# The attention residual of three row tiles: an identity product on TensorE, or a ScalarE copy and a GpSimd add

## The chip, the cores and the metric

The kernel runs on one core of a Trainium2 chip. Five engines share the core's on-chip memory (SBUF): TensorE (PE, matrix products, which write to PSUM), VectorE (DVE), ScalarE (ACT), GpSimd (POOL) and SyncE (SP, which here only issues transfers). Each works through its own instructions in the order of the program and waits on semaphores for the others. The metric is the device time of one execution in microseconds (us).

## The reference

A transformer block, forward only, on x of 2048 rows and 640 columns, followed by its gradients. The outputs are the block's result and the gradients of x and of all weights with respect to a given `grad_out`.

```python
x = A_x
h = x + _A_ref(_layernorm(x), A_wqkv, A_wo)      # linear attention, 32 heads of 20
h2 = h + _B_ref(_layernorm(h), B_w1, B_w3, B_w2) # silu(gate) * up, F = 1728
_out, _vjp = jax.vjp(_f, A_x, A_wqkv, A_wo, B_w1, B_w3, B_w2)
_grads = _vjp(grad_out)
```

The change is in how the first of the two residual sums, `h = x + attention`, is made for some of the rows. Matrix operands are bf16, sums in PSUM are f32, h is kept in bf16.

## The kernel before

The 2048 rows are 16 row tiles of 128 (`t` = 0 to 15), or 4 chunks of 512 rows (`c` = 0 to 3, four row tiles each). A row tile's 640 columns are handled in two halves of 320 (`j` = 0, 1; `HD` = 320).

The work is written in stages. The first makes q, k and the attention's small matrices. Then comes the stage that matters here: `f2_at` (line 634) makes the attention's result of a row tile, five matmuls per half into a PSUM tile `at` (line 642), adds x and writes h over x in `x_sb`. `ln2.part` (line 144) then takes statistics of that half (`bn_stats`, line 147), after the second half aggregates them (line 150), adds epsilon (line 153), and has GpSimd raise the sum to the power -0.5 (line 154). `f2_hn` normalizes the row tile on VectorE (line 160) and stores it; `f2_ht` transposes it for the MLP.

How x is added depends on the row tile:

- tiles 0 to 3, first half, tile 4, and tiles 8 to 15: VectorE adds x to the PSUM tile (line 649);
- tiles 0 to 3, second half, and tiles 5 to 7, both halves: a sixth matmul with the identity puts x into the PSUM sum (line 640), and ScalarE copies the sum to `x_sb` (line 647).

The MLP runs over the four chunks. `mlp(c, fc, between)` (line 762) does one of 14 column blocks: a matmul set of five for `gate`, one for `up`, and one for a later block of the gradient (`ghh_chunk`, line 390), each into a PSUM tile `mm` of which there are four. ScalarE empties them: sigmoid into `sig` and `s2` (lines 772, 773), copies into `up` and `gate` (lines 779, 783) and into `ghh` (line 406). These five SBUF tiles hold a pair of blocks. `sig`, `s2`, `gate` and `up` have two buffers each, so that ScalarE fills one pair while VectorE multiplies the other. For each pair VectorE does seven products or sums (line 808), queued in a list and let out one by one between other work. Three of their results go to DRAM (line 791): `hhT` by SP's queue, `gate` and `ghh` by GpSimd's queue, as `gg_d`. A `gate` buffer can be written again only when its store has landed.

While chunk c is multiplied, the row tiles of chunk c + 1 are prepared in between: `sides` (line 883) says after which block `f2_at`, `f2_hn` and `f2_ht` of each run. Tiles 5, 6 and 7 are therefore made in the first chunk, c = 0, in the blocks fc = 3, 6 and 8. The order of every engine's instructions is the order in which this program records them; no scheduler moves them.

The buffers of tag `h2` (two of 128 rows) serve several short-lived tiles: products of a row tile in the attention stage, the normalized rows of tile 3, and from chunk 1 on the block's results before they are stored.

Of the kernel before, what the change touches and what calls it, by code (L numbers as in the profile page):

```python
# [9 lines left out]
P = 128  # L10
BF16 = mybir.dt.bfloat16
F32 = mybir.dt.float32
ALU = mybir.AluOpType
# [10 lines left out]
W, SC, TPC = 512, 4, 4  # L24
HD = D // 2
# [30 lines left out]
def kernel(  # L56
# [19 lines left out]
    V, A, T, G, SY = nc.vector, nc.scalar, nc.tensor, nc.gpsimd, nc.sync  # L76
# [27 lines left out]
    def pool(name, side="left", space=None):  # L104
        kw = dict(space=space) if space is not None else dict(side=side)
        return tc.alloc_tile_pool(name=name, bufs=1, reuse_waits="tile", **kw)
# [68 lines left out]
    pf = pool("pf", "right")  # L175
# [457 lines left out]

    def f2_at(t, tag="at", halves=(0, 1), hold=False):
        for j in halves:
            on_pe = t < 2 * TPC and (t > TPC or (t < TPC and j == 1))
            at = ps.tile([P, 512], F32, name="at", tag=tag, bufs=2)
            xs = x_sb[:, t, j * HD:(j + 1) * HD]
            if on_pe:
                T.matmul(at[:, 0:HD], lhsT=ident[:], rhs=xs, start=True, stop=False)  # L640
            for c in range(DT):
                T.matmul(at[:, 0:HD], lhsT=pqT[:, c, t * P:(t + 1) * P], rhs=Wp[:, c, j * HD:(j + 1) * HD],  # L642
                         start=(c == 0 and not on_pe), stop=(c == DT - 1))

            def rest(at=at, xs=xs, j=j, on_pe=on_pe):
                if on_pe:
                    A.copy(out=xs, in_=at[:, 0:HD])
                else:
                    V.tensor_tensor(out=xs, in0=at[:, 0:HD], in1=xs, op=ALU.add)
                ln2.part(x_sb, t, j)  # L650

            at_rest.append(rest)
            if not hold:
                f2_rest()

    def f2_rest():
        while at_rest:
            at_rest.pop(0)()
# [185 lines left out]
    def f2_at0(t):  # L844
        f2_at(t, "o2")

    def f2_half(t, j, hold=False):
        f2_at(t, ("o2", "at")[t % 2], (j,), hold)
# [34 lines left out]
    def sides(c):  # L883
        side = ({}, {})
        for i in range(TPC):
            k0 = 3 * i - (i == TPC - 1) * (1 + (c == 1)) + (-2, 1, 0)[c]
            for k, pos, f in ((k0 + 2, 1, f2_at), (k0 + 3, 0, f2_hn), (k0 + 3, 1, f2_ht)):
                if c == 0 and f is f2_at:
                    if i == 0:
                        continue  # L890
                    f = f2_at0
                if k0 == -2 and f in (f2_at0, f2_hn, f2_ht):
                    k, pos = (k + 1, 0) if f is f2_at0 else (k + 1, pos)
                if k >= 0:
                    side[pos].setdefault(k, []).append((f, i))
        return side
# [610 lines left out]
```

## Time and profile before

| | |
|---|---|
| median of 3 runs | 823.75 us (823.6 to 826.96) |
| span of the profiled execution, first to last instruction | 821.9 us |
| the profiled execution's own time | not on the page beside its span; the median run is 1.85 us above that span |
| TensorE clock granted | 1.00 in every stretch looked at |
| PE busy | 814.4 us (99%) |
| DVE, ACT, POOL busy | 453.1 us (55%), 325.0 us (40%), 133.1 us (16%) |
| matmuls with the identity (line 640) | 10, of which 6 for tiles 5 to 7, at 107.1 to 125.2 us |
| ScalarE copies of tiles 5 to 7 (line 647) | 6, 0.425 to 0.606 us |

A line of the timeline has the start in us from the span's start, the duration, the engine, the source line, the operation, what it writes and reads, the shapes, and in brackets the engine's idle time before it with what ended it. "DMA gg_d<-gate" as releaser is the landing of a transfer. A line of a group has a count and the least, median and greatest duration in ns. Instructions of one engine overlap a little at their ends, so that starts are the better measure of their spacing. The page counts 5549 weight loads and 5522 matmuls; each matmul has its own load, so 27 matmuls have no record.

### The profile page before, as it was taken

How to read it: one execution, taken by the hardware profiler on the slowest of the kernel's cores; microseconds unless marked ns; L12 is line 12 of the kernel's file. 1: busy time of each engine (PE TensorE's matmuls, PEld its weight loads, DVE VectorE, ACT ScalarE, POOL GpSimd, SP SyncE). 2: the span in 40 equal slices, each digit the busy share in tenths (PEclk: the TensorE clock that was granted, in tenths of full speed). 3: DMA queues.
4: the chain of work that ended last, by engine and by line, in shares of the span. 5: the costliest groups of instructions: out<-in, count | busy, mean ns of one | idle time of the engine just before them, and what ended most of it. 6: DMA issues, size and time to landing. Idle time of an engine off the chain costs nothing.

```text
span 821.9 us, 14179 instructions
## 1 busy us (share of the span) xinstructions
PE 814.4 (99%) x5522; PEld 522.6 (64%) x5549; DVE 453.1 (55%) x961; ACT 325.0 (40%) x609; POOL 133.1 (16%) x194
## 2 busy tenths in 40 slices
PE   8999999999999999999999999999999999999998
PEld 6677544555555555777777777767777777555554
DVE  7869887999898566300057777772681545200000
ACT  7856688665565666011122212222212334211111
POOL 2243333323223212100001111110220000000000
PEclk9999999999999999999999999999999999999999
DMA  9999889696485556999677897258984898885771
GB/s 233 254 279 227 207 234 312 196 242 157 145 213 155 166 181 162 250 241 267 195 170 179 206 204 188 70 113 178 268 216 93 164 200 181 201 199 137 165 170 38
DMA packets 320883, 157.26 MB, mean 191 GB/s; under 512 B 238704, under 2 KB 314064, under 8 KB 320816
## 3 DMA queue, kind: packets, MB, share of 16 engines
q1 hardware_dynamic: 278768, 115.54, 61.3%
q0 software_dynamic: 7328, 24.48, 8.9%
q10 hardware_dynamic: 34720, 16.34, 8.7%
q8 instruction: 43, 0.70, 0.4%
q14 instruction: 24, 0.20, 0.1%
HBM read 47.01 MB, written 51.13 MB: 119 GB/s over the span
## 4 chain that ended last, share of the span: by engine, by line
PE 94%; DVE 2%; ACT 1%; DMA 1%; issue 0%; SPq 0%; POOL 0%; DVEq 0%; ACTq 0%
PE mm L386 20%; PE job L1271 20%; PE ghn L1070 14%; PE gxn L1429 8%; PE o L833 7%; PE gw L1025 7%; PE gwo L1155 3%; PE big L266 3%; PE gr L1127 3%; PE dkv L1375 3%; PE macc L416 2%; PE at L642 2%; DMA wqkv<-in_A_wqkv_dram 1%; PE dkv L1303 1%; DVE st L147 1%; DMA Wp<-pkx 1%
## 5 line engine op out<-in xcount | busy, mean ns | idle before, releaser
L1271 PE MATMUL job<-gb,hnN 128*128 128x432 bf16 (+2 forms) x656 | 117.0, 342 | 0.0
L1070 PEld LDWEIGHTS <-ggb 128*128 128x128 bf16 x864 | 84.5, 98 | 32.8
L1271 PEld LDWEIGHTS <-hnN 128*128 128x128 bf16 x656 | 63.6, 98 | 53.4
L386 PE MATMUL mm<-pqT,w 128*128 128x512 bf16 x397 | 93.1, 379 | 0.5
L386 PEld LDWEIGHTS <-w 128*128 128x128 bf16 x540 | 52.5, 98 | 63.1 <-issue 0.8
L1275 ACT CAST obs<-job 128x432 bf16<-128x432 f32 (+3 forms) x61 | 29.3, 480 | 123.1 <-PE job L1271 123.1
L833 PE MATMUL o<-w,hhT 128*128 128x320 bf16 x448 | 67.7, 299 | 0.1
L1070 PE MATMUL ghn<-w13a,ggb 128*128 128x320 bf16 x448 | 63.5, 299 | 0.0
L1070 PE MATMUL ghn<-w13b,ggb 128*128 128x320 bf16 x416 | 61.4, 299 | 0.0
L386 PE MATMUL mm<-g2T,w2T 128*128 128x512 bf16 x227 | 58.5, 379 | 0.6
L833 PEld LDWEIGHTS <-hhT 128*128 128x128 bf16 x448 | 43.8, 98 | 23.8 <-issue 0.2
L1025 PE MATMUL gw<-g,hb 128*128 128x320 bf16 x416 | 56.8, 299 | 0.0
L1135 POOL TENSOR_TENSOR sz<-Zb,g_h 128x640 f32<-128x640 bf16 x16 | 20.2, 1260 | 198.8 <-DVE g_h L1133 107.7
L1025 PEld LDWEIGHTS <-hb 128*128 128x128 bf16 x416 | 40.6, 98 | 16.0 <-issue 0.3
L1429 PE MATMUL gxn<-wqT,gT 128*128 128x320 bf16 x320 | 48.7, 299 | 0.0
L406 ACT CAST ghh<-mm 128x512 bf16<-128x512 f32 x48 | 28.3, 590 | 44.7 <-PE mm L386 39.0
L772 ACT ACTIVATE sig<-mm 128x512 bf16<-128x512 f32 x56 | 33.9, 605 | 25.1 <-PE mm L386 21.6
L1082 ACT ACTIVATE gs<-ghn 128x640 bf16<-128x640 f32 x16 | 11.2, 703 | 78.9 <-PE ghn L1070 73.4
L386 PEld LDWEIGHTS <-w2T 128*128 128x128 bf16 x260 | 25.4, 98 | 23.3
L266 PEld LDWEIGHTS <-pqT 128*128 128x128 bf16 x320 | 30.6, 98 | 14.4 <-issue 1.7
L1429 PEld LDWEIGHTS <-gT 128*128 128x128 bf16 x320 | 31.3, 98 | 12.2
L266 PE MATMUL big<-wqkv,pqT 128*128 128x320 bf16 x250 | 38.5, 299 | 0.3
(210 smaller groups left out, 1282.3 us busy)
## 6 DMA issues: line engine op xcount, KB each, us to landing
hh_d<-hhT SPq DMA_DIRECT2D x24, 256.0 KB, 2.8
gg_d<-gate POOLq DMA_DIRECT2D x24, 256.0 KB, 4.1
gg_d<-ghh POOLq DMA_DIRECT2D x24, 256.0 KB, 3.5
ggb<-gg_d SPq DMA_DIRECT2D x6, 896.0 KB, 5.4
ggb<-gg_d ACTq DMA_DIRECT2D x6, 832.0 KB, 5.7
out_dram<-obs ACTq DMA_DIRECT2D x39, 108.0 KB, 3.0
x_sb<-in_A_x_dram SPq DMA_DIRECT2D x6, 640.0 KB, 5.4
ggb<-gg_d SPq DMA_DIRECT2D x2, 1728.0 KB, 13.5
```

Of the source, the lines that this page charges most:

```text
L266: T.matmul(acc, lhsT=pqT[:, c, t * P:(t + 1) * P], rhs=wqkv[:, c, n0:n0 + HD], start=(c == 0), stop=(c == DT - 1))
L386: T.matmul(acc[:], lhsT=w[:, c, fc * P:(fc + 1) * P], rhs=rhs[:, c, :], start=(c == 0), stop=(c == DT - 1))
L406: A.copy(out=ghh[n // 2][:, n % 2, :], in_=acc[:])
L772: A.activation(sig[:, i, :], gp[:], AF.Sigmoid)
L833: T.matmul(o2["ps"][:, 0:HD], lhsT=hhT[c][:, fc, i * P:(i + 1) * P], rhs=w2[:, fc, j * HD:(j + 1) * HD], start=(fc == 0), stop=(fc == FT - 1))
L1025: T.matmul(acc[:, j, 0:HD], lhsT=hb[b][:, t, i * P:(i + 1) * P], rhs=g2[:, t, j * HD:(j + 1) * HD], start=(t == 0), stop=(t == ST - 1))
L1070: T.matmul(acc[:, j, 0:HD], lhsT=ggb[t // 2][:, k, lo:lo + P], rhs=rhs[:, j * HD:(j + 1) * HD], start=(k == 0), stop=(k == NG - 1))
L1127: T.matmul(gr[t][:, j, 0:HD], lhsT=ghT[t][:, c, :], rhs=wT2[:, c, j * HD:(j + 1) * HD], start=(c == 0), stop=(c == DT - 1))
L1155: T.matmul(acc[m][:, j, 0:n], lhsT=r_sb[:, t, m * P:(m + 1) * P], rhs=g_hx[:, t, j * HD:j * HD + n], start=(t == 0), stop=(t == ST - 1))
L1271: T.matmul(acc[:, 0:n], lhsT=lhs[:, t, m * P:(m + 1) * P], rhs=rhs(t), start=(t == 0), stop=(t == ST - 1))
L1275: A.copy(out=ob, in_=acc[:, 0:n])
L1429: T.matmul(acc[:, j, 0:HD], lhsT=g, rhs=wqT[:, k, j * HD:(j + 1) * HD], start=(k == 0), stop=(k == 14))
```

## The change

For row tiles 5, 6 and 7 the matmul with the identity is gone. ScalarE copies the PSUM sum of the attention alone, as f32, into a new tile `af`, which takes the buffers of tag `h2`. GpSimd adds `af` and x and writes h to `x_sb`. The rest, tiles 0 to 3 among it, stays. `G.tensor_tensor` is GpSimd's operation on two tiles, as `V.tensor_tensor` is VectorE's.

```diff
     def f2_at(t, tag="at", halves=(0, 1), hold=False):
         for j in halves:
-            on_pe = t < 2 * TPC and (t > TPC or (t < TPC and j == 1))
+            on_pe = t < TPC and j == 1
+            on_g = TPC < t < 2 * TPC
             at = ps.tile([P, 512], F32, name="at", tag=tag, bufs=2)
             xs = x_sb[:, t, j * HD:(j + 1) * HD]
             if on_pe:
...
-            def rest(at=at, xs=xs, j=j, on_pe=on_pe):
+            def rest(at=at, xs=xs, j=j, on_pe=on_pe, on_g=on_g):
                 if on_pe:
                     A.copy(out=xs, in_=at[:, 0:HD])
+                elif on_g:
+                    af = pf.tile([P, HD], F32, name="af", tag="h2", bufs=2)
+                    A.copy(out=af[:], in_=at[:, 0:HD])
+                    G.tensor_tensor(out=xs, in0=af[:], in1=xs, op=ALU.add)
                 else:
                     V.tensor_tensor(out=xs, in0=at[:, 0:HD], in1=xs, op=ALU.add)
                 ln2.part(x_sb, t, j)
```

## The prediction

> **What bounds the kernel now.** I read the page first, then the groups of instructions of the tiles that the change touches, then the timeline of each engine around row tiles 5 to 7, and last the busy time by stretches.
>
> ```profile
> span 821.9 us, 14179 instructions
> PE 814.4 (99%) x5522; PEld 522.6 (64%) x5549; DVE 453.1 (55%) x961; ACT 325.0 (40%) x609; POOL 133.1 (16%) x194
> PE 94%; DVE 2%; ACT 1%; DMA 1%; issue 0%; SPq 0%; POOL 0%; DVEq 0%; ACTq 0%
> ```
>
> TensorE (PE) is busy for 99% and carries 94% of the chain that ended last, so a matmul less is a gain of its issue time and a TensorE stall is a loss one for one. GpSimd (POOL) has 84% of its time free; what counts is who waits for it.
>
> The stretches (after the window: busy us of PE, weight loads, VectorE (DVE), ScalarE (ACT), POOL, each with its count; clock; DMA share; GB/s) show the cover behind the change:
>
> ```profile
> 98.00:120.00 22.00, 21.89 (x110) 10.87 (x111) 19.16 (x38) 16.39 (x33) 8.15 (x12) 1.00 0.87 216
> 120.00:142.00 22.00, 21.89 (x112) 10.48 (x113) 18.49 (x34) 18.80 (x39) 7.64 (x11) 1.00 1.06 308
> 142.00:164.00 22.00, 21.89 (x119) 11.65 (x119) 19.85 (x41) 15.06 (x28) 6.94 (x11) 1.00 0.67 212
> 164.00:186.00 22.00, 21.84 (x118) 11.71 (x120) 21.48 (x45) 13.44 (x25) 6.39 (x9) 1.00 0.93 241
> ```
>
> Tiles 5, 6 and 7 lie at 107, 116 and 124 us, in MLP chunk 0. VectorE has 2 to 4 us idle per 22 us there and half a microsecond from 164 to 186: what it loses it regains slowly. The clock is 1.00 throughout.
>
> The timeline of the three engines at tiles 5 to 7 (start, duration, engine, line, out<-in, idle before and its releaser):
>
> ```profile
> 110.06 0.71 POOL L791 DMA_DIRECT2D gg_d<-ghh  x1 [1.03 <-DVE ghh L808]
> 114.30 0.74 POOL L791 DMA_DIRECT2D gg_d<-gate  x1 [1.68 <-ACT up L779]
> 126.86 0.72 POOL L791 DMA_DIRECT2D gg_d<-gate  x1 [2.53 <-ACT x_sb L647]
> 133.84 0.72 POOL L791 DMA_DIRECT2D gg_d<-gate  x1 [3.33 <-ACT gate L783]
> ...
> 119.71 0.58 ACT L783 CAST gate<-mm 128x512 bf16<-128x512 f32 x1 [2.61 <-DMA gg_d<-gate]
> 120.19 0.76 ACT L647 CAST x_sb<-at 128x320 bf16<-128x320 f32 x2
> 140.32 0.58 ACT L783 CAST gate<-mm 128x512 bf16<-128x512 f32 x1 [0.84 <-DMA gg_d<-gate]
> ...
> 110.28 0.88 DVE L147 BATCH_NORM_STATS2 st<-x_sb 128x6 f32<-128x320 bf16 x2
> 111.19 0.21 DVE L150 BATCH_NORM_AGGREGATE ln_mv<-st 128x2 f32<-128x12 f32 x1
> 120.66 0.89 DVE L147 BATCH_NORM_STATS2 st<-x_sb 128x6 f32<-128x320 bf16 x2 [1.59 <-ACT x_sb L647]
> 126.83 0.88 DVE L147 BATCH_NORM_STATS2 st<-x_sb 128x6 f32<-128x320 bf16 x2
> ```
>
> Two ScalarE copies already wait for something in POOL's queue: `gate` at 119.71 and at 140.32 waits until the store of an earlier `gate` has landed, because that tile has two buffers. A store issued later makes those copies later by as much.
>
> **The change part by part.** It takes six identity matmuls from TensorE (one per half of tiles 5 to 7). ScalarE's six copies stay and write f32 into a buffer of tag h2, whose last readers were done before 102 us. It adds six GpSimd adds. The matmul sets, stores and copies keep their order on every queue; on POOL each pair of adds stands behind the `gg_d` store that precedes it, on VectorE the same `bn_stats` now waits for the adds.
>
> *Identity products.* In the timeline a 128x320 matmul follows the one before by 0.135 us (the identity at 107.08, the next at 107.21). Six times 0.135 is 0.81 us, four of them (0.54) before 117.9, two (0.27) after 124.
>
> *ScalarE's copies.* They took a median of 0.43 us with a bf16 output. With f32 no row shows them; the bound below is no change, the bound above the 128x512 copy's 0.59, which is 0.16 each. I take no change, as the input and the element count stay.
>
> *The add.* No row shows it. The nearest are these groups (median ns in the middle):
>
> ```profile
> L358 POOL TENSOR_TENSOR pr<-pql,Zb x8: 777/787/792, 67.3 to 85.7; 128x320 f32<-128x320 bf16 x8
> L1135 POOL TENSOR_TENSOR sz<-Zb,g_h x16: 1252/1260/1262, 424.8 to 551.4; 128x640 f32<-128x640 bf16 x16
> L649 DVE TENSOR_TENSOR x_sb<-at,x_sb x22: 474/476/491, 87.1 to 258.0; 128x320 bf16<-128x320 f32 x22
> ```
>
> From below 0.476 (VectorE's own add of the same size), from above 1.26 (GpSimd with twice the elements); I take 0.787, the same engine, shape and number of inputs.
>
> *Tile 5.* POOL issues the `ghh` store at 110.06 for 0.71, then the adds run from 110.80 to 111.59 and 112.38. `bn_stats` of the second half can start at 112.42 and takes 0.49; the aggregate moves from 111.19 to 112.92, so VectorE is 1.7 late. Behind it stands the product whose result the next `gate` store carries: 114.30 becomes 116.0. That store landed at 119.63 before; everything that shares the DMA engines with it is issued behind VectorE too, on SP's and POOL's queues alike, so I keep its 5.33 us: 121.35. ScalarE's `gate` at 119.71 becomes 121.43, and the copies queued behind it (two of tile 6, ghh, sig, s2, up) move with it, as ScalarE has no idle time until 126.
>
> *TensorE's stall.* The matmul set at 121.13 uses the PSUM buffer that this `gate` copy releases (at 120.30, 0.83 before). Without four identities TensorE is there at 120.59 and waits for 122.02 plus 0.07: 0.97 late. The set at 122.21 waits for the ghh copy (end 121.45, then 123.17): 1.03 late. The set at 123.29 waits for the up copy (end 122.92, then 124.64): 1.42 late. Tile 7's two identities give 0.27 back: 1.15.
>
> *Tile 6.* Its copies end at 120.63 and 120.96 before, 122.35 and 122.68 after; the adds run to 124.02, the aggregate moves from 121.58 to 124.56: VectorE is 3.0 late. Its idle 1.59 us there was ScalarE's wait, which moves along.
>
> *Tile 7.* The `gate` store at 126.86 moves by 3.0 to 129.86, 0.72 later the adds start, they end at 132.2, and the aggregate moves from 127.75 to 132.76: 5.0 late. VectorE waits for these two adds over 2 us, with seven products of the next pairs queued behind.
>
> *What is late next.* The pair's product into ghh (128.78 to 129.47) ends at 134.5 and releases the s2 buffer that ScalarE wants at 133.3 (132.13 plus 1.15); TensorE had 1.0 us in hand, 0.26 more late: 1.41. VectorE's idle 0.71 us ahead of 130.54 absorbs as much, 4.3 remain. The store at 133.84 becomes 138.1, lands after its 6.4 us at 144.5 (140.24 before), and the `gate` copy at 140.32 ends at 145.2. TensorE's set at 141.88 had 0.98 in hand behind it and starts at 145.27: 3.39 late. In chunk 1 VectorE has almost no idle time; a PSUM tile that VectorE empties at 191.5 had 0.16 us in hand: I add 0.5 for this and a smaller such wait near 158.
>
> *Sum.* -0.81 (identities) + 1.96 (122 to 125 us) + 0.26 + 1.98 (145 us) + 0.5 = +3.9 us. The profiled execution has a span of 821.9 us; the median run is 823.75, 1.85 above, which I leave as it is. So 821.9 + 3.9 + 1.85 = 827.65, or 0.47% more. Each pair of adds is in line three times on the way to the store at 138.1, so a microsecond on one add is up to six: 0.476 gives +2.0, 1.26 gives +6.7. 0.16 on each ScalarE copy would be at most 0.3 per tile, 0.9 in all.
>
> The Trainium skill (GPSIMD Engine Reference, Engine selection) advises against this placement: an elementwise add of two tiles belongs on VectorE, GpSimd being about twice as slow. The rows above give 1.65 times (0.787 against 0.476). By the page's factor an add would be 0.95 as an estimate, and the sum +4.9 instead of +3.9. It prices the instruction alone; here the wait behind the queue costs more than the ratio.
>
> **The rivals.**
>
> *Only the first stall costs* (0.17). VectorE's lateness is made up before 133.84, so that only tile 5's effect reaches TensorE: +1.15, 824.9 us. For it: 2 to 4 us of idle time per stretch. Against: 5.0 late at 127.75 and only 0.71 idle ahead of that store.
>
> *The waits are hidden and the identities are the whole effect* (0.10): -0.81, 822.9 us, on the other side. Place: the store at 114.30. It landed in 5.33 us at a DMA share of about 1, while others of the same size took 3.5 to 3.7. Issued at 116.0 and landed in 4.2 it would be there at 120.2, within what TensorE has in hand (0.83 plus 0.54). It decides as long as both waited-for stores land 1.1 us or more sooner after their issue; the second, at 6.4, would need to come down to 3.1, which speaks against it.
>
> *The add is slower than its rows* (0.13): an f32 and a bf16 input, with VectorE and DMA descriptors beside it. At 1.1 to 1.3 us the sum is +5.8 to +7.0, some 830.2 us. For it: POOL's one-element power took 0.55 us alone and 0.93 beside VectorE's products. Against: while the adds run VectorE stands at the statistics.
>
> That the change does not do what it says is excluded: six adds and six f32 copies stand in the order of the changed program.
>
> **How the numbers follow.** The case worked out has 0.55, with a range of its own from 826.2 to 828.9 (an add between 0.55 and 1.0 us, at six per us); 0.05 is left for anything else. 0.5% is 4.1 us, about what a measurement here tells from no change, and the bound is 827.9, almost at the forecast: of the 0.55, 0.25 lies above and 0.30 below. Slower: 0.25 + 0.13 + 0.02 = 0.40. Same: 0.30 + 0.17 + 0.08 + 0.02 = 0.57. Faster: 0.03, a hidden wait with a luckier stretch behind it. The range 824.2 to 830.2 leaves out the hidden case and half of the slow add, under 2 in 10.
>
> **What would show it.** In the changed profile: six POOL adds of 0.79 us; `bn_stats` of tiles 5 to 7 preceded by VectorE idle time released by POOL (about 1.4 to 2.3 us each); ScalarE's `gate` waits for the store at about 121 and, 3 to 4 us long, at about 144; TensorE gaps just ahead of 122 and 145 us of 1 to 2 us each; from 150 us on every row some 4 us later. Wrong would be: adds away from 0.79, stores that land sooner when issued later, or VectorE catching up before 140.

## The result, and the profile after

The changed kernel takes 827.14 us (median of 6 runs, 826.42 to 829.31) against 823.61 us for the kernel before (6 runs on the same chip). The ratio is 1.0041, with a 95% interval from 1.0029 to 1.0054: 3.4 us slower, 2.4 to 4.4. The prediction was 827.65, a ratio of 1.0047, so the time lies in its range and in the case that was taken as the likeliest: slower by less than 0.5%. (0.5% is 4.1 us, and the interval reaches just past it.) The profiled execution took 826.95 us with a span of 825.2 (821.9 before).

From the page after: the span, the engines' busy time and the chain that ended last.

```profile
span 825.2 us, 14176 instructions
...
PE 815.3 (99%) x5516; PEld 523.0 (63%) x5543; DVE 453.1 (55%) x961; ACT 324.7 (39%) x609; POOL 137.7 (17%) x200
...
PE 86%; DVE 7%; DMA 2%; issue 2%; ACT 2%; POOL 1%; DVEq 0%; ACTq 0%; POOLq 0%
```

Six matmuls fewer and 4.6 us more on POOL, as the change says. The chain now leaves TensorE for longer: TensorE carried 94% of it and now 86%; VectorE has 7% instead of 2%, DMA and issue 2% each instead of 1% and 0%. These are shares of a path and not time lost: 8% of the span would be 66 us, and the loss is 3.4.

The groups of tile `af` after, with least, median and greatest duration in ns:

```profile
L651 ACT COPY af<-at x6: 431/462/595, 108.4 to 128.4; 128x320 f32<-128x320 f32 x6
L652 POOL TENSOR_TENSOR x_sb<-af,x_sb x6: 743/761/784, 110.8 to 131.5; 128x320 bf16<-128x320 f32 x6
```

An add is 0.76 us, 1.6 times VectorE's 0.476. ScalarE's copy into f32 is 0.46 where the bf16 one had a median of 0.43 in the kernel before.

The timelines of POOL, VectorE, ScalarE and TensorE after (in brackets the idle time before and its releaser; lines left out are marked):

```profile
110.84 1.45 POOL L652 TENSOR_TENSOR x_sb<-af,x_sb 128x320 bf16<-128x320 f32 x2
...
115.70 0.74 POOL L796 DMA_DIRECT2D gg_d<-gate  x1 [1.43 <-DVE gate L813]
...
122.69 1.54 POOL L652 TENSOR_TENSOR x_sb<-af,x_sb 128x320 bf16<-128x320 f32 x2 [1.32 <-ACT af L651]
...
130.82 1.47 POOL L652 TENSOR_TENSOR x_sb<-af,x_sb 128x320 bf16<-128x320 f32 x2
...
138.14 0.73 POOL L796 DMA_DIRECT2D gg_d<-gate  x1 [2.53 <-ACT s L778]
...
111.62 0.49 DVE L147 BATCH_NORM_STATS2 st<-x_sb 128x6 f32<-128x320 bf16 x1 [1.25 <-POOL x_sb L652]
...
123.51 0.49 DVE L147 BATCH_NORM_STATS2 st<-x_sb 128x6 f32<-128x320 bf16 x1 [2.79 <-POOL x_sb L652]
...
131.62 0.49 DVE L147 BATCH_NORM_STATS2 st<-x_sb 128x6 f32<-128x320 bf16 x1 [1.50 <-POOL x_sb L652]
...
121.69 0.59 ACT L788 CAST gate<-mm 128x512 bf16<-128x512 f32 x1 [3.06 <-DMA gg_d<-gate]
...
144.14 0.59 ACT L788 CAST gate<-mm 128x512 bf16<-128x512 f32 x1 [3.19 <-DMA gg_d<-gate]
...
122.32 1.24 PE L386 MATMUL mm<-g2T,w2T 128*128 128x512 bf16 x5 [1.47 <-ACT gate L788]
...
124.94 1.24 PE L386 MATMUL mm<-pqT,w 128*128 128x512 bf16 x5 [0.23 <-ACT up L784]
...
144.78 2.32 PE L386 MATMUL mm<-pqT,w 128*128 128x512 bf16 x10 [1.27 <-ACT gate L788]
...
195.00 1.52 PE L643 MATMUL at<-Wp,pqT 128*128 128x320 bf16 x10 [0.31 <-DVE rden L365]
```

Read it from top to bottom as one chain. POOL's adds end; the statistics of tiles 5, 6 and 7 have waited 1.25, 2.79 and 1.50 us for the first of each pair (and 0.2 to 0.3 us for the second); of the 2.79, 1.59 was a wait for ScalarE before. VectorE is late, so the `gate` stores are issued at 115.70 and 138.14 instead of 114.30 and 133.84. ScalarE's `gate` copies wait 3.06 and 3.19 us for those stores to land. TensorE, which never waited in this stage before, waits 1.47, 0.23 and 1.27 us for the PSUM buffers that these copies empty. The last line is a small one of its own in chunk 1, 0.31 us behind VectorE. (L796, L788 and the like are the lines of the changed kernel, five further down than in the kernel before.)

The stretches after (window, then busy us of PE, weight loads, VectorE, ScalarE, POOL with counts; clock; DMA share; GB/s) show that it is idle time and not slower work:

```profile
98.00:120.00 22.00, 21.89 (x108) 10.67 (x109) 18.63 (x37) 16.16 (x32) 8.97 (x13) 1.00 0.80 192
120.00:142.00 22.00, 20.19 (x101) 9.34 (x102) 16.76 (x32) 16.98 (x35) 10.47 (x14) 1.00 0.96 257
142.00:164.00 22.00, 20.62 (x109) 10.76 (x110) 18.68 (x38) 14.28 (x27) 6.41 (x10) 1.00 0.79 262
```

TensorE's busy time falls from 21.89 to 20.19 and 20.62 in the second and third stretch, at a clock of 1.00. (The page's total for PE is no measure of this: two runs below with spans of 822.9 and 822.6 us have totals of 814.0 and 815.6.)

To see where time goes, one more reading helps: the start of the same TensorE instruction in the two timelines, after minus before, at the time that the instruction had before. It is +0.10 us at 99 us (a difference from ahead of the change; in the runs below it is -0.3 to +0.9), -0.44 at 118, +1.65 at 123, +1.38 at 126, +1.46 at 134, +2.90 at 142, +3.37 from 192 to the end. Such differences are called "shift" below, counted from their value at 99 us.

### The profile page after: what moved, and what is told of

It is laid out like the page before. It is cut to its first block, busy times and chain, and to the rows that moved or that the text cites. A ratio compares the mean times of both kernels' runs of the same rounds, so it can differ in the third digit from the quotient of the medians.

```text
span 825.2 us, 14176 instructions
## 1 busy us (share of the span) xinstructions
PE 815.3 (99%) x5516; PEld 523.0 (63%) x5543; DVE 453.1 (55%) x961; ACT 324.7 (39%) x609; POOL 137.7 (17%) x200
## 4 chain that ended last, share of the span: by engine, by line
PE 86%; DVE 7%; DMA 2%; issue 2%; ACT 2%; POOL 1%; DVEq 0%; ACTq 0%; POOLq 0%
PE job L1276 19%; PE ghn L1075 14%; PE mm L386 12%; PE gxn L1434 8%; PE gw L1030 7%; PE o L838 6%; PE big L266 3%; PE gwo L1160 3%; PE dkv L1380 3%; PE gr L1132 3%; PE macc L416 2%; DMA gg_d<-gate 1%; PE at L643 1%; DVE s L813 1%; DVE gate L813 1%
```

## The experiments

The theory: the adds cost nothing as work on POOL; they cost because VectorE, working in order, waits for them at the statistics with the product behind it that feeds a `gate` store, and from there through the landing of the store to ScalarE's `gate` copy and TensorE's PSUM buffers. The main rivals: the six adds disturb by running at all (descriptors, ports, DMA); or a late store costs nothing by itself, and the loss comes from something else that is late.

**The identities alone.** The kernel before without the six identity products. It leaves out x from h in the rows of tiles 5 to 7.

```diff
+            ident_mm = on_pe and t < TPC
...
-            if on_pe:
+            if ident_mm:
```

> The kernel before without the six identity products of tiles 5 to 7; the x of these rows is left out of h, the rest stays. My theory: TensorE issues 0.81 us less, four of the six reach it ahead of the set at 123.29, which has to wait for ScalarE's up copy some 0.2 us, so -0.6 us (-0.8 to -0.4) against the kernel before. Rival: the identities are hidden behind ScalarE or VectorE anyway, 0.0 us. If the rival holds, the whole +3.4 of the change are waits; if my theory holds, the waits cost about 4.0 and the identities give part of it back.

Measured: ratio 0.9988 (0.9975 to 1.0002), which is -1.0 us and by its interval alone not apart from no change. The trace is sharper: TensorE's shift falls from tile to tile to -0.71 at 126 us and stays. The term of 0.81 us in the sum holds to 0.1, though the run's own expectation was -0.6, and TensorE gets a saved matmul nearly in full.

**The adds without a wait.** The identities stay, and six GpSimd adds are put in the same places, whose results nobody reads.

```diff
                     A.copy(out=xs, in_=at[:, 0:HD])
+                    if t > TPC:
+                        af = pf.tile([P, HD], F32, name="af", tag="h2", bufs=2)
+                        G.tensor_tensor(out=af[:], in0=xs, in1=xs, op=ALU.add)
```

> The kernel before with identities and copies as they are, and six GpSimd adds of 128x320 in the same places of POOL's queue, which write to tiles that nobody reads. VectorE does not wait for them; GpSimd is busy for as long and at the same moments as in the changed kernel. My theory (VectorE's wait is what costs): the power of the statistics is queued behind the adds, so VectorE's normalization is 0.6 us later for tile 5 and 0.7 for tile 7; +0.4 us (0 to +0.8). Rival (GpSimd's adds themselves slow VectorE's products or the stores' descriptors): +3.4 us or more, as in the changed kernel.

Measured: ratio 1.0005 (0.9993 to 1.0017), +0.4 us. The adds as work on POOL are not the 3.4 us. (Five took 0.71 to 0.73 us, one 1.26; VectorE waits 0.46 us for the power behind the first pair, is about 1 us late and has made it up by 121.) The trace is not without loss: TensorE has no gap at 122 us, but its shift rises by 0.4 up to 142 us, by 0.5 at 192 and by 0.35 at 206; that execution took 825.21 us where the median is 824.93.

**The wait with a little work ahead of it.** In the changed kernel the statistics of tiles 5 to 7 are recorded behind the next two products, where these are still to do, and the normalization behind one more.

```diff
-                ln2.part(x_sb, t, j)
+                if on_g:
+                    late.append((t, j))
+                else:
+                    ln2.part(x_sb, t, j)
...
+        if late:
+            while late:
+                ln2.part(x_sb, *late.pop(0))
+            drain(1)
+            between()
```

> The changed kernel, with the statistics of tiles 5 to 7 moved behind the next two of VectorE's products (1.2 to 1.4 us of work), and one more product between the statistics and the normalization. Adds, copies and stores stay where they are. My theory: VectorE's wait for the adds falls from 1.5, 1.5 and 1.7 us to some 0.4 each, the fifth pair's gate store is 1 to 2 us late instead of 4.3; +1.0 us against the kernel before (0 to +2.0). Rival (the place of VectorE's wait does not matter, as the two adds behind the gate store set the pace): +3.4 us, unchanged.

Measured: ratio 1.0014 (1.0003 to 1.0025), +1.2 us: two thirds of the loss go with the place of the wait, with the same adds, copies and transfers. The TensorE gap at 122 is gone, and at 126 us the shift is -0.83, the identities' whole gain. What takes it back begins at 129.5, as ScalarE's and TensorE's timelines show:

```profile
128.85 0.59 ACT L798 CAST gate<-mm 128x512 bf16<-128x512 f32 x1 [4.38 <-DMA gg_d<-gate]
...
129.49 1.24 PE L386 MATMUL mm<-g2T,w2T 128*128 128x512 bf16 x5 [1.10 <-ACT gate L798]
```

This is another store than in the changed kernel: the third pair's, issued at 120.29 and landed 8.5 us later, where it took 5.8 (issued at 120.66) and stopped nothing. So what is left here is not a remainder of the changed kernel's two gaps.

**The wait taken away.** The statistics go behind three or four products, and the normalization, its store and the transposition of these tiles one block later.

```diff
+        while late:
+            ln2.part(x_sb, *late.pop(0))
...
+                elif c == 0 and i > 0:
+                    k += 1
```

> The changed kernel, with the statistics of tiles 5 to 7 moved behind three to four of VectorE's products, and each tile's normalization, store and transposition one MLP block later. My theory: by then the adds are done, VectorE no longer waits, the gate stores of the second and fifth pair are not later than in the kernel before, and what is left is the gain of the identities: -0.8 us (-1.2 to 0.0) against the kernel before. Rival (the adds cost something wherever VectorE waits, through GpSimd's queue ahead of the power and the stores): +1 us or more.

Measured: ratio 1.0007 (0.9997 to 1.0018), +0.6 us: the loss is gone, but so is the expected gain. VectorE's timeline of this kernel shows where the gain went:

```profile
111.08 1.24 DVE L819 TENSOR_TENSOR s<-gate,s 128x1024 bf16<-128x1024 bf16 x1
112.36 1.12 DVE L819 TENSOR_TENSOR gate<-gate,ghh 128x1024 bf16<-128x1024 bf16 x1
113.40 0.88 DVE L147 BATCH_NORM_STATS2 st<-x_sb 128x6 f32<-128x320 bf16 x2
...
121.13 2.03 DVE L819 TENSOR_TENSOR ghh<-s,ghh 128x1024 bf16<-128x1024 bf16 x1
...
128.66 1.97 DVE L819 TENSOR_TENSOR ghh<-s,ghh 128x1024 bf16<-128x1024 bf16 x1
```

No line has an idle time before it, yet the products that lie beside a pair of adds take 1.24 and 1.12, 2.03, and 1.97 us instead of 0.69. VectorE loses about 1.0, 1.3 and 1.3 us all the same, as stretched work where the changed kernel has a wait. TensorE's shift is -0.82 at 126 us, the whole gain, and then 1.18 us are lost at one place, 142 us, behind a `gate` copy that waited 2.40 us for its store: the fifth pair's, issued at 135.31 and landed 5.9 us later. So the second of the two waits is not quite taken away. My expectation (-0.8) had taken a product beside an add at its usual length.

**Each add twice.** x is added twice for tiles 5 to 7, so that a pair of adds becomes four.

```diff
-                    G.tensor_tensor(out=xs, in0=af[:], in1=xs, op=ALU.add)
+                    G.tensor_tensor(out=af[:], in0=af[:], in1=xs, op=ALU.add)
+                    G.tensor_tensor(out=xs, in0=af[:], in1=xs, op=ALU.add)
```

> The changed kernel with each of the six adds done twice (x is added two times in the rows of tiles 5 to 7), so that VectorE's wait per tile grows by two adds, 1.5 us. My theory: VectorE's lateness adds up over three tiles, 4.3 becomes 8.8 us at the fifth pair's gate store, and TensorE follows: +8 us against the kernel before (+6.5 to +10, the upper end if the longer gap costs clock). Rival (a fixed disturbance of the order, not the length of the wait): +3.4 us, as in the changed kernel.

Measured: ratio 1.0126 (1.0109 to 1.0142), +10.4 us. The direction and much of the size are as expected: the same waits, longer. But it is no clean measure of the price per microsecond, since the clock gave way. TensorE's timeline and two stretches of it:

```profile
124.06 1.24 PE L386 MATMUL mm<-g2T,w2T 128*128 128x512 bf16 x5 [2.31 <-ACT gate L789]
125.21 3.98 PE L386 MATMUL mm<-pqT,w 128*128 128x512 bf16 x10
```

```profile
124.00:130.00 6.00, 5.94 (x23) 2.53 (x23) 2.65 (x7) 4.18 (x10) 4.05 (x5) 0.72 1.07 305
130.00:136.00 6.00, 6.00 (x31) 2.83 (x29) 3.61 (x7) 5.41 (x11) 3.09 (x5) 1.00 0.76 184
```

After the gap of 2.31 us, ten matmuls took 3.98 us instead of 2.32, at a granted clock of 0.72 over six microseconds. The same comes a second time: after a gap of 2.04 us at 140.93, behind an `up` copy, five matmuls took 2.07 us instead of 1.24 and ten took 3.22 instead of 2.32, and the clock from 142 to 148 us was again 0.72. Together that is about 3.4 of the 7 us on top of the changed kernel's loss; the other 3.6, by this estimate, are longer waits, about 4.8 us for each microsecond on one add, where the prediction has "up to six".

**Only the stores late, by dead adds ahead of them.** In the kernel before, two adds nobody reads stand on POOL ahead of the second pair's `gate` store and five ahead of the fifth pair's; VectorE waits for none of these adds.

```diff
+                late = {1: 2, 4: 5}.get(k, 0) if c == 0 and r0 == F else 0
+                for _ in range(late):
+                    af = pf.tile([P, HD], F32, name="af", tag="h2", bufs=2)
+                    G.tensor_tensor(out=af[:], in0=out[:, 0, 0:HD], in1=out[:, 1, 0:HD], op=ALU.add)
```

> The kernel before, identities and all, with nothing for VectorE to wait for; two GpSimd adds on dead data stand just ahead of the gate store of the second pair (114.30 us) and five ahead of the fifth pair's (133.84), each reading what that store sends, so that the stores are issued 1.5 and 3.8 us later. My theory (store, then the buffer of gate, then ScalarE, then PSUM): TensorE stalls ahead of 122 us until it is 1.4 us late and ahead of 145 until it is about 2.9 late; +2.9 us in all (+2.0 to +3.8). Rival (VectorE's lateness reaches TensorE by another way, the stores had time in hand): under +0.7 us.

Measured: ratio 1.0074 (1.0050 to 1.0099), +6.1 us, twice the expectation, for three reasons. First, the dead adds ran beside VectorE's products and took 1.16 us each instead of 0.76. Second, they began late: the third pair's store, issued at 120.70 instead of 119.01, landed after 9.4 us instead of 5.7, a `gate` copy waited 4.14 us for it, VectorE waited 4.21 us for the copy of tile 7 behind that, and TensorE had gaps of 0.59 and 0.23 us at 131 to 133. So the fifth pair's store came at 142.77, 8.9 us late instead of 3.8 (0.85 of it is the offset of the two profiles). Third, TensorE then stood still for over 4 us behind the `gate` copy, which had waited 6.29 for that store, and the clock fell. TensorE's timeline, and the stretch that followed:

```profile
148.46 3.62 PE L386 MATMUL mm<-pqT,w 128*128 128x512 bf16 x10 [4.37 <-ACT gate L783]
```

```profile
148.00:154.00 6.00, 5.54 (x21) 2.56 (x21) 2.67 (x5) 5.50 (x11) 0.00 (x0) 0.72 0.57 221
```

The second pair's store, though 2.6 us late (116.89), landed 2.6 us after its issue, where it took 5.3 before, in time for a copy at 119.58: no gap at 122. A late store can stop TensorE, but need not.

**The fifth pair's store alone.** The same with three dead adds ahead of the fifth pair's store and none elsewhere.

> The kernel before with one change: three GpSimd adds on dead data stand ahead of the gate store of the fifth pair, each reading what that store sends, so that this store alone is issued some 3 us later (1.17 us an add beside VectorE's products, as measured, less the 0.5 that the store waits anyway). VectorE waits for no add. My theory: the gate copy at 140.32 comes 3 us later, TensorE has 1 us in hand and stands for 2 us ahead of 142; +2.2 us in all (+1.2 to +3.2). Rival (the store's lateness only matters together with VectorE's own): under +0.7 us. If a standing TensorE also loses clock, as in the longer wait of the two late stores, the gap costs more than its length, some +3.5.

Measured: ratio 1.0007 (0.9998 to 1.0016), +0.6 us: my expectation failed, and the rival it names holds. POOL's timeline, and the answer on that store with the time from issue to landing:

```profile
133.55 3.49 POOL L812 TENSOR_TENSOR af<-gate 128x320 f32<-128x320 bf16 x3 [3.50 <-ACT up L779]
136.98 0.73 POOL L791 DMA_DIRECT2D gg_d<-gate  x1
```

```profile
DMA to landing us min/median/max: 2.6/2.6/2.6
```

The store was issued 3.14 us late and landed in 2.6 us instead of 6.4, a little earlier than before. What had kept it in the kernel before seems to be not its own transfer but what was in front of it: a w2 load of 640 KB, issued by SP at 132.90, one microsecond ahead. In this kernel that load keeps its time (132.53, landed 6.0 us later) and is 4.5 us ahead of the store. In the changed kernel it does not keep its time: SP issues it behind the store of `hhT`, which waits for VectorE, so load and store are late together (137.54 and 138.14). The load in SP's queue, before and after:

```profile
132.90 0.48 SPq L938 DMA_DIRECT2D w<-in_B_w_dram  x1
...
137.54 0.51 SPq L943 DMA_DIRECT2D w<-in_B_w_dram  x1
```

This would be why the prediction's "lands after its 6.4 us" came out nearly right, 5.9, where a store that alone is late lands far sooner. (TensorE does lose 0.9 us in this trace, at 146 to 148, behind a `ghh` copy that waited 2.64 us: the fifth pair's `ghh` store stands behind the late `gate` store in POOL's queue.)

**The load out of the store's way.** A direct test: the changed kernel with that load issued two column blocks (one pair) later, in one transfer with the next, and the kernel before with the same edit as control.

```diff
-            if c == 0 and fc in (5, 7, 9, 11):
-                a, b = {5: (0, 3), 7: (3, 6), 9: (6, 10), 11: (10, 13)}[fc]
+            if c == 0 and fc in (5, 7, 11):
+                a, b = {5: (0, 3), 7: (3, 6), 11: (6, 13)}[fc]
```

> The changed kernel, with one transfer moved: the w2 load of four blocks (640 KB), which SP issues at 137.54 us, just ahead of the fifth pair's gate store at 138.14, is issued together with the next w2 load, one block later (about 141.4). Theory (the landing of that store is set by the load queued in front of it, and the second TensorE gap by that landing): the store lands some 3 us after its issue instead of 5.9, about 141 to 142; ScalarE's gate copy no longer waits over 3 us for it, TensorE's gap of 1.27 us ahead of 144.8 goes, and the time is +2.0 us (1.2 to 2.8) against the kernel before instead of +3.4. Rival (VectorE's and ScalarE's lateness alone would hold TensorE there, whatever the store does): the gap comes back at the ghh or s copies, +3.0 to +3.6 us.

> The kernel before with the same load moved from 132.9 to about 138.6 us, as the control. Theory: TensorE had 0.98 us in hand behind that store, so nothing is gained: 0 us (-0.4 to +0.4). If the moved load alone is worth something (a rival to the reading of the run on the changed kernel), it is -0.5 us or more here.

Measured: the changed kernel with the load moved has a ratio of 1.0083 (1.0069 to 1.0096), +6.8 us; the kernel before with it 1.0021 (1.0010 to 1.0032), +1.7 us. Both miss the expected time. But the link in question is shown. The answers on the fifth pair's store, in the changed kernel and with the load moved, and after them ScalarE's and TensorE's timeline with the load moved:

```profile
L796 POOL DMA_DIRECT2D gg_d<-gate x1: 727/727/727, 138.1 to 138.1; - x1
...
  ACT gate L788: 3.2, 1
...
DMA to landing us min/median/max: 5.9/5.9/5.9
```

```profile
L796 POOL DMA_DIRECT2D gg_d<-gate x1: 725/725/725, 139.2 to 139.2; - x1
...
  ACT gate L788: 0.6, 1
...
DMA to landing us min/median/max: 3.3/3.3/3.3
```

```profile
142.65 0.58 ACT L788 CAST gate<-mm 128x512 bf16<-128x512 f32 x1 [0.61 <-DMA gg_d<-gate]
...
151.10 0.30 PE L838 MATMUL o<-w,hhT 128*128 128x320 bf16 x1 [3.52 <-DMA w<-in_B_w_dram]
```

With the load out of its way the store lands in 3.3 us, the copy waits 0.6 instead of 3.2 us, and TensorE's gap at 145 is gone (its shift stays at +1.7 us across 142, where the changed kernel's rises by 1.44). The control agrees: in the kernel before with the load moved, the same store lands in 3.1 us instead of 6.4. What the expectations left out is who needs the load: the first output product of chunk 1, at about 147 us. Moved, the load landed at about 151, and TensorE waited 3.52 us for it. The control says the same in small: a gap of 0.85 us at 145.55 for the load in place of no gap. So a later load is no way to have the second TensorE gap back; an earlier one was not tried.

**Single tiles.** The change for tile 5 alone, and for tile 7 alone.

```diff
-            on_pe = t < 2 * TPC and (t > TPC or (t < TPC and j == 1))
+            on_g = t == 5
+            on_pe = not on_g and t < 2 * TPC and (t > TPC or (t < TPC and j == 1))
```

> The change for tile 5 alone; tiles 6 and 7 keep their identity products. My theory: VectorE is 1.66 us late from 111 us on, the gate copy at 119.71 comes 1.7 to 2.0 later, TensorE is some 1.4 late by 125; VectorE has 0.7 idle at 130 and is under 1 us late for the fifth pair, which TensorE has in hand; +1.4 us in all (+0.8 to +2.0), with no gap ahead of 145. Rival (the whole loss comes from the last tile's adds, behind the gate store of 130): 0.0 us or below.

> The change for row tile 7 alone (tiles 5 and 6 keep their identities and bf16 copies). Theory: VectorE is 2.0 us late at 127.8, its idle 0.71 us takes some of it, the fifth pair's store is 1.3 late, of which TensorE had 0.98 in hand; two identities give 0.27: +0.2 us (-0.3 to +0.8). With tile 5 alone at +3.4, the losses of the single tiles then do not share the loss of the whole. Rival (each tile costs a third): +1.1 us; second rival (a single tile costs what all three cost, wherever it is): +3.4 us.

Measured: tile 5 alone 1.0041 (1.0028 to 1.0055), +3.4 us, as much as all three; tile 7 alone 1.0003 (0.9994 to 1.0012), +0.2 us. The first is a miss. TensorE's timeline with tile 5 alone:

```profile
118.42 0.30 PE L641 MATMUL at<-x_sb,ident 128*128 128x320 bf16 x1 [1.62 <-DMA x_sb<-in_A_x_dram]
...
144.93 2.32 PE L386 MATMUL mm<-pqT,w 128*128 128x512 bf16 x10 [0.45 <-ACT gate L788]
```

Here the first gap is another one: tile 6's identity product needs x, and the load of x for tiles 6 and 7 is in SP's queue behind the store of `hhT`, which waits for VectorE (issued 114.86 instead of 112.67, of which 0.6 us is the offset of the two profiles at 99 us). In the full change tile 6's identity is gone, only the add needs x, later, and TensorE does not meet this wait. The wait for x is 1.6 to 1.8 of the 3.4 us; the shift rises again by 0.6 at 142, behind the fifth pair's store, and by 0.5 at 192. With tile 7 alone VectorE is 1.8 us late at 128, a `gate` copy at 141.07 waits 1.85 us for its store, and TensorE has nearly that much in hand: its shift rises by 0.1 there. The losses of single tiles thus do not add up to the loss of the whole.

**The other way without the identity.** VectorE adds x straight from PSUM in the same places, as it does for tiles 8 to 15.

```diff
-            on_pe = t < 2 * TPC and (t > TPC or (t < TPC and j == 1))
+            on_pe = t < TPC and j == 1
```

> The kernel before, but VectorE adds x of tiles 5 to 7 straight from PSUM (0.476 us each), with no identity product, no ScalarE copy and no GpSimd. Theory (what costs is VectorE's lateness, 1.7, 1.4 and 2.0 us of waiting per tile; here it is late by the two adds alone, 0.95 us per tile less what its idle time takes, while ScalarE is relieved of 2.6 us): identities -0.8, waits +0.4 to +1.8 us, together +0.3 us (-0.4 to +1.0). Rival (VectorE has no time to give in this stage, so any work put on it is paid in full): -0.8 + 2.9 = +2.1 us.

Measured: ratio 1.0001 (0.9992 to 1.0010), +0.1 us, with the theory and against the rival. The adds are on VectorE and cost it 0.48 us each (two of the eight are tile 4's), and TensorE waits once in chunk 0:

```profile
L649 DVE TENSOR_TENSOR x_sb<-at,x_sb x8: 474/478/485, 98.8 to 128.4; 128x320 bf16<-128x320 f32 x8
```

```profile
121.82 1.24 PE L386 MATMUL mm<-g2T,w2T 128*128 128x512 bf16 x5 [0.95 <-ACT gate L783]
```

One hand-over fewer (no ScalarE copy, no POOL) makes VectorE 1.1 us late at 111 and 1.7 at 128 instead of 1.7 and 5.1, and the gain of the identities nearly pays for it (shift +0.3 from 126 to 205 us; a wait of 0.40 us for a transposed tile follows at 207). No version tried that adds x once in every row is shown to be faster than the kernel before.

## Why the prediction was right

*The sum, term by term*, from the shifts of the changed kernel:

| term | predicted | measured |
|---|---|---|
| identities before 118 us | -0.54 | -0.54 |
| TensorE's gaps at 121 to 125 us | +1.96 | +2.09 |
| tile 7's identities | -0.27 | -0.27 |
| s2 buffer, about 134 us | +0.26 | +0.08 |
| gap at 142 to 145 us | +1.98 | +1.44 |
| chunk 1 | +0.5 | +0.48 |
| sum | +3.9 | +3.3 |

*The add.* 0.787 us was taken from POOL's row with two bf16 inputs; it measured 0.761. Here the mixed f32 and bf16 input cost nothing extra. The rival of a slow add falls, for this place: VectorE stood at the statistics. Where the experiments put VectorE's products beside the adds, 1.16 and 1.26 us were seen, so the rival named a real effect that the change happens to avoid.

*The Trainium skill (GPSIMD Engine Reference, Engine selection)*, weighed in the prediction, gave by its factor of about 2 an estimated add of 0.95 us and a sum of +4.9; the trace has 1.6 times and +3.4. Its advice, VectorE for such an add, was right here (+0.1 us with VectorE's adds), for a reason that it does not price: the wait.

*VectorE's lateness.* Predicted 1.7, 3.0, 5.0 and 4.3 us; its shifts at 111, 123, 128 and 130 us, as compared in the timelines, are 1.7, 3.2, 5.1 and 4.3.

*The term that was mis-sized*, "The store at 133.84 becomes 138.1, lands after its 6.4 us at 144.5": it was issued at 138.14 and landed after 5.9 us, which makes 0.5 us of the 0.54 by which 1.98 was too much. The assumption behind it, that everything in front of the store is as late as the store, is right to that half microsecond; the runs with the store alone late and with the load moved show that the landing time depends on what is in front and not on the store alone. The prediction had the assumption from the order of the queues and no row for it: with the load on its time, as in the run with the store alone late, the store would have landed sooner.

*The rivals.* Only the first stall: excluded, the second gap is there (1.27 us). The waits hidden, identities the whole effect: the place named was the store at 114.30, landing 1.1 us or more sooner after its issue. It was issued at 115.70 and landed 5.9 us later (121.61), later than before and not sooner. The run with the statistics moved well back comes close to that rival's conditions and shows the -0.8 us up to 126 us.

*What was wrong behind a right sum.* The sentence "a microsecond on one add is up to six" treats the three tiles as alike and their losses as added. Tile 5 alone costs 3.4 us, as much as the whole, about half of it by a wait for x that the full change does not have, and tile 7 alone 0.2. The full change's loss is the chain as worked out, not three times a tile's. And 0.5% was not "about what a measurement here tells from no change": the interval reaches a microsecond to either side, a quarter of the 4.1 us, and tells the 3.4 us from nothing.

*What stays open.* The gap of 0.3 us in chunk 1, a step of 0.48 us at 192, returns with 0.48 to 0.50 in the runs with the adds beside, with late statistics and with single tiles (0.39 with each add twice), and not in the others with dead adds; that VectorE's lateness there is the remains of the first chunk's was argued, and no run tested it alone. Of the chunk's 0.5 in the sum, the smaller wait near 158 did not come. For the first gap no run moved the transfers in front of the second pair's store alone.

## What to carry to other kernels

An operation moved to an idle engine is priced by who waits for it in order: here six adds that nobody waits for cost 0.4 us, within the error of the measurement, and the same adds ahead of an in-order engine's next instruction 3.4, with the identities' gain already taken off. When a store is late, ask which loads in front of it are late by the same cause, since its landing can be theirs; and before such a load is moved out of the way, look up who needs its data first. The loss of a part of a change can be as large as that of the whole, so a part's number is not a share.

## What the runs showed of the hardware

*GpSimd adds and VectorE products hardly run side by side.* A 128x1024 product on VectorE took 0.69 us alone, 2.03 and 1.97 beside a pair of GpSimd adds (1.5 us together); an add took 0.76 us while VectorE waited, and 1.16 in the mean beside products. The 1.3 us that these two products lost are nearly the pair's length, as if VectorE had been held until the adds were done. The Trainium skill (SBUF — State Buffer, Who interferes with whom) has as a rule that a VectorE instruction with two SBUF inputs contends with a GpSimd instruction that reads SBUF, since its second input comes through a read interface that the two share, and it calls the shared ports an exclusive lock. These rows agree. It means that taking the wait away could not have won the wait's whole time.

*A store's landing depends on what is in front.* The fifth pair's `gate` store, always the same bytes, landed 6.4 us after its issue in the kernel before, 5.9 in the changed one, 3.3 and 3.1 with the load moved, and 2.6 when it alone was late. The second pair's goes the same way in all fourteen profiles: with SP's load of x 1.4 to 1.6 us ahead of it (before, after, VectorE's adds, single tiles and others) it landed after 4.8 to 6.1 us, with that load 2.1 us or more ahead (the adds beside, both kinds of later statistics, the two late stores) after 2.6 to 3.3. So the first gap, too, needs the load and the store late together, which is what VectorE's lateness does; for this store it is read from the traces and was not tested by moving the load.

*The clock after gaps.* Behind TensorE gaps of 2.31, 2.04 and 4.37 us the granted clock was 0.72 over six microseconds, and ten matmuls took 3.98, 3.22 and 3.62 us instead of 2.32. Behind the gap of 3.52 us for the w2 load it stayed at 1.00, as it did behind the changed kernel's 1.47. The length of a single gap does not decide it in these rows; the changed kernel's gaps were all without this extra price.
